# Attention, expert layer and gated layer in one kernel: routing and a weight conversion moved into the last sixth of each attention head

## Chip, cores and metric

One core of one Trainium2 chip. The metric is device time of one execution in microseconds, lower is better; the median of the runs shown is compared. The profile is one separate execution, taken with the hardware profiler.

## What is computed

Three stages, each feeding the next. All inputs are float32 except the three weights of the last stage, which reach the kernel as float64 and are read as pairs of 32-bit words.

```python
# 1 attention: 4 batches x 8 heads, 1152 keys, 64 wide, queries averaged in pairs (576)
scores = (q_pool @ k.T) / 8;  attn = softmax(scores);  x = attn @ v          # x: 2304 x 512
# 2 experts: each token goes to one of 8
e_idx = argmax(x @ w_gate);  gate_w = softmax(x @ w_gate)[e_idx]
out[mask] = gate_w * sigmoid(x @ w_output_gate)[e] * (relu(x[mask] @ w1[e]) @ w2[e])
# 3 gated layer, 1536 wide
out = (silu(x @ w_gate2) * (x @ w_val2)) @ w_out2
```

Outputs are float32. Matrix products are made in float32r, each operand split in a high and a low part (`hi`, `lo`), three products for one.

## The kernel before

Line numbers are those of the profile.

**Attention (32 heads).** A head takes nine blocks of 128 keys. For each, TensorE makes the scores `sb` (L432), ScalarE the exponential `a` (L439), ScalarE or VectorE the high part `ah` (L448), VectorE or GpSimd the low part `al` (L452: GpSimd for blocks 0, 1, 2 and 8), and three blocks later TensorE adds `o` (L470). In the same stretch TensorE and VectorE find the next head's row maxima (`sa` L393, `MX` L397, finished by `m` L402 and placed by `tm` L415), and ScalarE, GpSimd and TensorE prepare the head after that (`ks`, `qs`, `qd`, `vl`, `tk`, `tq`). `sa`, `sb`, `tq`, `tk`, `tx` and the small products of the routing share three PSUM buffers (`ps2`). The order on every engine is written out by hand: the loop over `it` gives each piece a block and a place in it, and `merge` sorts them. Lists that have no fixed place are spread over a fraction of the head.

**Routing.** When the eight heads of a batch are done, `route` makes, on 96 partitions with 6 tokens each, the expert of each token, its rank within the expert (five additions that run along the six tokens, L551, and a product with a triangular matrix, `rk` L556 and L557), the weight, and a row in a table in DRAM, `tbl_d`. Six indirect DMAs on GpSimd's queue write the rows (`put`, L586). `first_steps` then makes `step_e`, the table of the first six expert steps, from three batches. The pieces of batches 0, 1 and 2 are spread evenly over whole heads, 0.02 to 0.98, in heads 9 to 15, 17 to 23 and 25 to 28. Batch 3 is routed during the first three expert steps.

**Start of the experts.** After head 29's pieces (`it == n - 3`), `start_experts` reads `step_e` into registers on SP's queue, loads the token lists `mt` (L134), gathers the tokens of steps 0 and 1 with two indirect DMAs on GpSimd's queue (`xg`, L139), and loads two experts' weights (L150).

**Expert steps.** 23 sure steps of 128 tokens: products `h` (L180), relu `hs`, transposes `t`, products `y` (L899), scaling `ys` (L907), and a scatter to `y_d` on GpSimd's queue (L908). A further group stands behind a branch on a register (L1007), which these inputs do not take.

**Gated layer.** `p` (L1070) over 12 chunks of 128 columns, two at a time, and `o` (L1095). `narrow` turns 128x512 float64 values into float32 by word operations (L236 to L253): four tensor-scalar passes and one two-input pass on VectorE, two activations on ScalarE, two passes on GpSimd. The first two chunks' six units are converted in the last expert steps, in `W1`'s unused buffer as scratch (tile name `W`); what is left of them follows the loop as `after` and stands ahead of the branch. The other 30 units are converted during the gated layer. Loads of `y_d` (L1046) wait for all scatters.

```python
        for ops, slots in zip(made, (tail(2, 8, 12), tail(1, 0, 4), tail(1, 4, 12), tail(0, 0, 12))):
            spread([(0, fn) for fn in ops], slots)
        after = sum(made[4:], [])
```

Of the kernel before, what the change touches and what calls it, by code (L numbers as in the profile page):

```python
# [8 lines left out]
F32 = mybir.dt.float32  # L9
# [28 lines left out]
def kernel(  # L38
# [42 lines left out]
    wide = moe2_w_gate.dtype == I64  # L81

# [10 lines left out]
    iota_e = rt.tile([QP, QT, E], F32, name="iota_e")  # L93
    ebase = rt.tile([QP, QT, E], F32, name="ebase")
# [121 lines left out]
    def narrow(f, part, tile_, to):  # L216
# [21 lines left out]
        ts = nc.vector.tensor_scalar  # L238
        act = nc.scalar.activation
# [10 lines left out]
            lambda: nc.vector.scalar_tensor_tensor(  # L250
                out=t["e"], in0=t["hi"], scalar=-0x80000000, in1=t["e"], op0=ALU.bitwise_and, op1=ALU.bitwise_or
            ),
            lambda: nc.gpsimd.tensor_tensor(out=t["w"], in0=t["w"], in1=t["e"].bitcast(F32), op=ALU.mult),  # L253
# [4 lines left out]
    with ExitStack() as actx:  # L258
# [6 lines left out]
        dup_p = early("dup", 2)  # L265
        one = pool("one", 1)
# [23 lines left out]
        zrow = one.tile([1, DM], F32, name="zrow")  # L290
# [227 lines left out]
        def route(b, ps):  # L518
            s = gs[b]
            G = [QP, QT, E]  # L520
# [6 lines left out]
            lg = rt.tile([QP, QT, 2 * E], F32, name="lg")  # L527
            lo = lg[:, :, 0:E]
            mx = rt.tile([QP, QT, 1], F32, name="gmx")
            d = rt.tile(G, F32, name="gd")  # L530
            ex = rt.tile(G, F32, name="gex")
            oh = rt.tile(G, F32, name="goh")
            mi = rt.tile([QP, QT, 1], F32, name="gmi")
            run = rt.tile(G, F32, name="grun")
            z = rt.tile(G, F32, name="gz")
            ze = rt.tile([QP, QT], F32, name="gze")
            sume = rt.tile([QP, QT], F32, name="gsum")
            meta = rt.tile([QP, QT, 2], I32, name="meta")
            s["oh"], s["meta"] = oh, meta
            flat = lambda t: t.rearrange("p t e -> p (t e)")  # L540
            do(lambda: V.tensor_reduce(out=lg, in_=s["lp"], axis=AX.X, op=ALU.add))
            do(lambda: V.tensor_reduce(out=mx, in_=lo, axis=AX.X, op=ALU.max))

            do(lambda: V.tensor_tensor(out=oh, in0=lo, in1=mx.to_broadcast(G), op=ALU.is_ge))
            do(lambda: V.tensor_tensor(out=oh, in0=oh, in1=iota_e, op=ALU.mult))
            do(lambda: V.tensor_reduce(out=mi, in_=oh, axis=AX.X, op=ALU.min))
            do(lambda: V.tensor_tensor(out=oh, in0=iota_e, in1=mi.to_broadcast(G), op=ALU.is_equal))
# [6 lines left out]
            def ranks():  # L554
                s["rk"] = ps([128, QT * E], "rk")
                nc.tensor.matmul(s["rk"][:QP, :], tri, flat(oh), start=True, stop=False)  # L556
                nc.tensor.matmul(s["rk"][:QP, :], ones, flat(run), start=False, stop=True)  # L557

            do(lambda: V.tensor_tensor(out=d, in0=lo, in1=mx.to_broadcast(G), op=ALU.subtract))
            do(lambda: V.tensor_tensor(out=z, in0=lg[:, :, E:2 * E], in1=oh, op=ALU.mult))  # L560
            do(lambda: V.tensor_reduce(out=ze, in_=z, axis=AX.X, op=ALU.add))
# [5 lines left out]
            do(lambda: V.tensor_reduce(out=sume, in_=ex, axis=AX.X, op=ALU.add))  # L567
            do(lambda: V.tensor_scalar(out=sume, in0=sume, scalar1=1e-9, scalar2=None, op0=ALU.add))
            do(lambda: V.reciprocal(out=sume, in_=sume))
            s["ranks_at"] = len(ops)  # L570
            do(ranks)
            do(lambda: nc.gpsimd.iota(meta[:, :, 0], pattern=[[1, QT]], base=b * SQ, channel_multiplier=QT))
            do(lambda: V.tensor_tensor(out=meta[:, :, 1].bitcast(F32), in0=ze, in1=sume, op=ALU.mult))

            def place():
                sl = rt.tile(G, F32, name="gsl")
                nc.vector.tensor_tensor(out=sl.rearrange("p t e -> p (t e)"), in0=s["rk"][:QP, :], in1=ebase.rearrange("p t e -> p (t e)"), op=ALU.add)
                nc.vector.tensor_tensor(out=sl, in0=sl, in1=s["oh"], op=ALU.mult)
                sf = rt.tile([QP, QT], F32, name="gsf")
                nc.vector.tensor_reduce(out=sf, in_=sl, axis=AX.X, op=ALU.add)  # L580
                si = rt.tile([QP, QT], U32, name="gsi")
                nc.vector.tensor_copy(out=si, in_=sf)
                s["si"] = si

            def put(t):
                i = nc.gpsimd.indirect_dma_start(  # L586
                    out=tbl_d[:, :], out_offset=bass.IndirectOffsetOnAxis(ap=s["si"][:, t:t + 1], axis=0),
# [6 lines left out]
            do(place)  # L594
            for t in range(QT):
                ops.append((500, lambda t=t: put(t)))
            return ops

# [119 lines left out]
        with tc.manual_schedule():  # L718
# [9 lines left out]
            for o, src in ((D + 1, moe_w_gate), (D + 1 + E, moe_w_output_gate)):  # L728
# [8 lines left out]
            nc.vector.memset(zrow, 0.0)  # L737
            nc.gpsimd.memset(tri, 1.0)
            nc.gpsimd.affine_select(
                out=tri, in_=tri, pattern=[[1, QP]], compare_op=ALU.is_gt, fill=0.0, base=0, channel_multiplier=-1  # L740
            )
            fl = nc.gpsimd
            fl.iota(iota_e, pattern=[[0, QT], [1, E]], base=-E, channel_multiplier=0, allow_small_or_imprecise_dtypes=True)
            fl.iota(ebase, pattern=[[0, QT], [NT, E]], base=0, channel_multiplier=0, allow_small_or_imprecise_dtypes=True)
# [9 lines left out]
            nc.sync.dma_start(out=x_d[NT:NT + 1, :], in_=zrow)  # L754
# [7 lines left out]
            pending, events = [], {}  # L762
# [6 lines left out]
            for it in range(-2, n + 1):  # L769
# [29 lines left out]
                if 0 < it < n and it % 2 == 0:  # L799
                    b = (it - 1) // H  # L800
                    if it % H == 0:
                        ops = route(b, ps_a)
                        if b == B - 2:
                            ops += first_steps(ps_a)
# [397 lines left out]
```

## Time and profile before

| | us |
|---|---|
| median of 3 runs (1378.57 to 1382.09) | 1381.45 |
| profiled execution, its own time | 1384.52 |
| its span | 1382.8 |
| PE busy (share of the span) | 1321.7 (96%) |
| DVE busy | 999.7 (72%) |
| ACT busy | 853.7 (62%) |
| POOL busy | 616.0 (45%) |
| PE's share of the chain that ended last | 82% |

The span has three parts: attention up to about 592, experts up to about 895, the gated layer from about 919. A busy share is a mean over parts with different limits; TensorE is the engine to look at in all three, and what counts is where it stands still or runs at the lower of its two clocks.

### The profile page before, as it was taken

Reading aid. Unit: us, or ns where it says so; the run is one execution under the profiler, and the core shown is the slowest. Engines: PE = TensorE matmul, PEld = TensorE weight load, DVE = VectorE, ACT = ScalarE, POOL = GpSimd, SP = SyncE. Lnnn points to the kernel's source line nnn. Section 1 sums busy time; section 2 is a strip of 40 time slices with the busy share of each in tenths; the row PEclk is TensorE's granted clock in tenths of the full one; section 3 lists DMA queues with packets and bytes.
Section 4 is the critical chain, followed back from the end, with each engine's and each line's share of the span. In section 5 each row is a group of like instructions: output and inputs, shape, how many; then the busy total and the mean of one; then the engine's idle time right before and its main releaser. Section 6 shows DMA issues by size and latency. Waiting matters only on the chain.

```text
span 1382.8 us, 22804 instructions
## 1 busy us (share of the span) xinstructions
PE 1321.7 (96%) x8392; PEld 1225.2 (89%) x8392; DVE 999.7 (72%) x1608; ACT 853.7 (62%) x1366; POOL 616.0 (45%) x510
## 2 busy tenths in 40 slices
PE   7999999999999999998999999759999999999998
PEld 6999999999998989877888888549999999999998
DVE  5888888878888898789888888855545555555533
ACT  6888888778876877887888988434332323232211
POOL 7666666676667675306354455521211222122100
PEclk9999999999999999999999999869999999999999
DMA  5333443334333431713545255233111101111011
GB/s 142 87 86 90 109 102 85 82 78 120 87 87 87 121 69 27 276 42 107 184 144 212 79 186 207 94 115 107 39 46 46 46 31 46 47 46 32 16 63 75
DMA packets 96261, 129.58 MB, mean 94 GB/s; under 512 B 47760, under 2 KB 60176, under 8 KB 95762
## 3 DMA queue, kind: packets, MB, share of 16 engines
q1 hardware_dynamic: 91698, 117.31, 29.5%
q0 software_dynamic: 4448, 10.77, 2.3%
q8 instruction: 68, 1.11, 0.4%
q14 instruction: 47, 0.39, 0.1%
HBM read 154.46 MB, written 15.64 MB: 123 GB/s over the span
## 4 chain that ended last, share of the span: by engine, by line
PE 82%; DVE 6%; DMA 5%; issue 3%; ACT 2%; POOL 1%; SPq 0%; POOLq 0%; DVEq 0%
PE p L1070 22%; PE o L470 13%; PE o L1095 11%; PE sb L432 9%; PE h L180 7%; PE y L899 7%; PE sa L393 6%; DMA y_d<-ys,mt 2%; PE tx L493 2%; DVE MX L397 2%; DMA W<-in_moe_w_dram 1%; DVE ah L448 1%; PE tk L367 1%; PE t L888 1%; PE tq L346 1%
## 5 line engine op out<-in xcount | busy, mean ns | idle before, releaser
L397 DVE TENSOR_REDUCE MX<-sa 128x1 f32<-128x576 f32 (+1 forms) x320 | 233.3, 751 | 54.1 <-PE sa L393 50.3
L439 ACT ACTIVATE a<-sb 128x576 f32<-128x576 f32 x288 | 187.8, 652 | 105.3 <-PE sb L432 98.2
L452 POOL TENSOR_TENSOR al<-a,ah 128x576 fp32r<-128x576 f32 x124 | 176.4, 1433 | 131.0 <-DVE ah L448 121.3
L1070 PE MATMUL p<-yh,ah 128*128 128x384 f32 x576 | 195.8, 340 | 0.7 <-ACT yh L1059 0.7
L1070 PE MATMUL p<-yl,ah 128*128 128x384 f32 x576 | 194.4, 338 | 0.0
L1070 PE MATMUL p<-yh,al 128*128 128x384 f32 x576 | 193.9, 337 | 0.0
L470 PE MATMUL o<-ah,vh 128*65 128x288 f32 x576 | 173.8, 302 | 1.2 <-ACT oT L480 1.2
L470 PE MATMUL o<-al,vh 128*65 128x288 f32 x576 | 171.2, 297 | 1.4 <-DVE al L452 1.3
L470 PE MATMUL o<-ah,vl 128*65 128x288 f32 x576 | 170.4, 296 | 0.0
L452 DVE TENSOR_TENSOR al<-a,ah 128x576 fp32r<-128x576 f32 x164 | 141.4, 872 | 20.7 <-ACT ah L448 20.7
L1079 DVE TENSOR_TENSOR u<-p,u 128x384 f32<-128x384 f32 x72 | 40.1, 557 | 147.6 <-PE p L1070 147.6
L393 PE MATMUL sa<-KA,TA 128*128 128x288 f32 (+2 forms) x640 | 142.2, 307 | 4.6 <-DVE MX L397 2.0
L248 POOL TENSOR_TENSOR w<-w,cx 128x512 f32<-128x512 f32 x30 | 38.8, 1295 | 231.2 <-ACT cx L246 231.2
L157 DVE TENSOR_TENSOR w1l<-W,w1h 128x1024 fp32r<-128x1024 f32 x92 | 116.7, 1290 | 23.8 <-ACT w1h L156 19.5
L448 ACT CAST ah<-a 128x576 fp32r<-128x576 f32 x195 | 131.8, 676 | 2.9
L432 PE MATMUL sb<-TA,KA 128*128 128x288 f32 x576 | 125.2, 300 | 0.7 <-DVE MX L397 0.4
L432 PE MATMUL sb<-TB,KB 128*128 128x288 f32 x576 | 124.3, 297 | 0.0
L156 ACT CAST w1h<-W 128x1024 fp32r<-128x1024 f32 x92 | 96.9, 1054 | 33.7 <-PE h L180 29.2
L1070 PEld LDWEIGHTS p<-yh,ah 128*128 128x128 f32 x576 | 108.9, 189 | 4.0 <-ACT yh L1059 1.1
L1070 PEld LDWEIGHTS p<-yh,al 128*128 128x128 f32 x576 | 108.8, 189 | 2.8
L1070 PEld LDWEIGHTS p<-yl,ah 128*128 128x128 f32 x576 | 108.7, 189 | 0.2 <-DVE yl L1060 0.2
L393 PEld LDWEIGHTS sa<-KA,TA 128*128 128x128 f32 (+2 forms) x640 | 98.7, 183 | 11.3 <-DVE MX L397 6.0
(213 smaller groups left out, 3168.8 us busy)
## 6 DMA issues: line engine op xcount, KB each, us to landing
W<-in_moe_w_dram SPq DMA_DIRECT2D x42, 2048.0 KB
kr<-in_k_dram SPq DMA_DIRECT2D x32, 288.0 KB
qr<-in_q_dram SPq DMA_DIRECT2D x32, 288.0 KB
vr<-in_v_dram SPq DMA_DIRECT2D x32, 288.0 KB
KB<-KA SPq DMA_DIRECT2D x31, 288.0 KB
W<-in_moe_w_dram SPq DMA_DIRECT2D x16, 512.0 KB
rb<-in_moe_w_gate_dram SPq DMA_DIRECT2D x10, 512.0 KB
rb<-in_moe_w_val_dram SPq DMA_DIRECT2D x10, 512.0 KB
```

What stands on the lines that cost most here:

```text
L156: nc.scalar.copy(out=hi, in_=W1[p % 2][:, c, :])
L157: nc.vector.tensor_tensor(out=lo, in0=W1[p % 2][:, c, :], in1=hi.bitcast(F32), op=ALU.subtract)
L180: nc.tensor.matmul(s["h"][:, g * 512:(g + 1) * 512], x_[:, c, :], w[:, g * 512:(g + 1) * 512], start=(c == 0 and i == 0), stop=(c == DC - ...
L393: nc.tensor.matmul(ps[:w, c, 0:S // 4], TA[j][0:K_, t * 128:t * 128 + w], KA[j][0:K_, c0:c0 + S // 4], start=True, stop=True,)
L397: nc.vector.tensor_reduce(out=mx[:w, t, hf:hf + 1], in_=ps[:w, :, 0:S // 4], axis=AX.XY, op=ALU.max)
L432: nc.tensor.matmul(ps[:, hf, 0:SQ // 2], w[j][:, c * 128:(c + 1) * 128], t[j][:, hf * (SQ // 2):(hf + 1) * (SQ // 2)], start=first, stop=n ...
L439: nc.scalar.activation(out=a.rearrange("p (a b) -> p a b", a=2), in_=ps[:, :, 0:SQ // 2], func=AF.Exp, scale=0.5 / float(D) ** 0.5,)
L448: (nc.scalar.copy if HI_ACT[c] or i == n - 1 else nc.vector.tensor_copy)(out=ah, in_=a)
L452: (nc.gpsimd if LO_POOL[c] and i < n - 1 else nc.vector).tensor_tensor(out=al, in0=a, in1=ah.bitcast(F32), op=ALU.subtract)
L470: nc.tensor.matmul(s["o", hf][:D + 1, 0:SQ // 2], s[w][:, c, :], s["a"][c][x][:, hf * (SQ // 2):(hf + 1) * (SQ // 2)], start=(c == 0 and p ...
L1070: nc.tensor.matmul(p_, w[:, g, c, :], y_[:, c, :], start=(c == 0 and i == 0), stop=(c == DC - 1 and i == 2),)
L1095: nc.tensor.matmul(ob[t][i], t_[:, ts], w, start=(first and j == 0), stop=(last and j == 2))
```

## The change

1. Conversion of the six early units: each is fetched at the start of head 0, 3, 6, 9, 12 or 15 and converted in three pieces, in the last sixth (0.84 to 0.99) of that head and of the next two, then written to a DRAM tensor `w_d`. The last expert steps only load the finished float32 chunks (`load_chunk`); `after` is gone.
2. `narrow` itself (early units and the 30 later ones): the two GpSimd passes become two VectorE passes, and one activation is folded into one of them.
3. Routing of batches 0 and 1 together, 12 tokens a partition: `sums` at the end of heads 8 and 16, `route` over heads 18 to 21, the twelve `put`s over heads 22 to 25. Batch 2: heads 25 to 27, its six `put`s and `first_steps` over heads 28 and 29. All of it in 0.84 to 0.99 of a head. The running count is one scan in place of copies and additions.
4. Small edits: constants without repetition, a tensor `going` for the scan, the row of zeros of `x_d` from `fill`, no `anew`.

```diff
+    w_d = dram.tile([GF, 128, 3 * DM], F32, name="w_d") if wide else None
...
             lambda: ts(out=t["e"], in0=t["e"], scalar1=896.0, scalar2=0.0, op0=ALU.subtract, op1=ALU.max),
-            lambda: nc.gpsimd.tensor_tensor(out=t["w"], in0=t["w"], in1=t["x"], op=ALU.add),
             lambda: ts(out=t["e"], in0=t["e"], scalar1=254.0, scalar2=float(1 << 23), op0=ALU.min, op1=ALU.mult),
...
-            lambda: nc.gpsimd.tensor_tensor(out=t["w"], in0=t["w"], in1=t["e"].bitcast(F32), op=ALU.mult),
+            lambda: stt(
+                out=t["w"], in0=t["lo"].bitcast(U32), scalar=2.0 ** -52, in1=t["w"], op0=ALU.mult, op1=ALU.add),
+            lambda: nc.vector.tensor_tensor(out=t["w"], in0=t["w"], in1=t["e"].bitcast(F32), op=ALU.mult),
...
-            do(lambda: V.tensor_copy(out=run[:, 0, :], in_=cnt))
-            for t in range(1, QT):
-                do(lambda t=t: V.tensor_tensor(out=run[:, t, :], in0=run[:, t - 1, :], in1=oh[:, t - 1, :], op=ALU.add))
-            do(lambda: V.tensor_tensor(out=cnt, in0=run[:, QT - 1, :], in1=oh[:, QT - 1, :], op=ALU.add))
+            do(lambda: V.tensor_tensor_scan(
+                out=flat(by_e[1]), data0=flat(going[nb - 1]), data1=flat(by_e[0]), initial=0.0, op0=ALU.mult, op1=ALU.add))
+            if b:
+                do(lambda: V.tensor_tensor(out=run, in0=run, in1=per_e(cnt.unsqueeze(1)), op=ALU.add))
+            do(lambda: V.tensor_copy(out=cnt, in_=run[:, T - 1, :]))
...
-                lists = [(pending.pop(0), 0.02, 0.98)] if pending else []
+                lists = []
...
-                        at_, m = gs[b]["ranks_at"], 4 if b == B - 2 else H - 1
-                        cuts = [len(ops) * i // m for i in range(m + 1)]
-                        cuts = [at_ + 4 if at_ < c < at_ + 4 else c for c in cuts]
-                        pending += [ops[a:c] for a, c in zip(cuts, cuts[1:])]
+                if 0 < it < n and it % H == 0:
+                    b = it // H - 1
+                    j, nb = (b, 2) if b < 2 else (0, 1)
+                    rest(it, [(200, lambda: sums(b, j, nb))])
+                    if b == 1:
+                        ops, puts = route(0, 2, ps_a)
+                        over(it + 2, 4, ops)
+                        over(it + 6, 4, puts)
+                    if b == 2:
+                        ops, puts = route(2, 1, ps_a)
+                        over(it + 1, 3, ops)
+                        over(it + 4, 2, puts)
+                        over(it + 4, 2, first_steps(ps_a))
+                if it % 3 == 0 and 0 <= it // 3 < len(units):
+                    f, part = units[it // 3]
+                    fetch, ops, t = narrow(f, part, early_tile, lambda: P["c"].tile([128, DM], F32, name="cw"))
+                    fetch()
+                    ops.append(lambda t=t, f=f, part=part: nc.sync.dma_start(
+                        out=w_d[f, :, part * DM:(part + 1) * DM], in_=t["w"]))
+                    for i, (a, c) in enumerate(((0, 3), (3, 6), (6, len(ops)))):
+                        rest(it + i, [(1, op) for op in ops[a:c]])
+                lists.append((extra.pop(it, []), 0.84, 0.99))
...
+        if wide and f < GF:
+            nc.sync.dma_start(out=r, in_=w_d[f, :, part * DM:(part + 1) * DM])
...
-        for ops, slots in zip(made, (tail(2, 8, 12), tail(1, 0, 4), tail(1, 4, 12), tail(0, 0, 12))):
-            spread([(0, fn) for fn in ops], slots)
-        after = sum(made[4:], [])
+        spread(
+            [(0, lambda f=f, part=part: load_chunk(f, part)) for f in range(GF) for part in range(3)],
+            [(p, c) for p in range(NSURE - 3, NSURE) for c in (4, 5)])
...
-            for fn in after:
-                fn()
```

Three places in the order. The first is VectorE at the end of head 1, where the second piece of a converted unit now stands (`ce` is the exponent word, `rb` the raw words). Before:

```order
L402 TENSOR_REDUCE m<-MX_133 128x5
L452 TENSOR_TENSOR al<-a,ah 128x576 x3
L448 CAST ah<-a 128x576
L397 TENSOR_REDUCE MX_134<-sa 128x1 x5
```

In the change:

```order
L403 TENSOR_REDUCE m<-MX_139 128x5
L453 TENSOR_TENSOR al<-a,ah 128x576 x2
L247 TENSOR_SCALAR ce<-ce 128x512
L248 TENSOR_SCALAR ce<-ce 128x512
L249 SCALAR_TENSOR_TENSOR ce<-rb,ce 128x512
L453 TENSOR_TENSOR al<-a,ah 128x576
L449 CAST ah<-a 128x576
L398 TENSOR_REDUCE MX_140<-sa 128x1 x5
```

A piece now stands between the second and the third `al` of the group, ahead of the cast and of the next head's row maxima.

The second place is where head 29 ends and `start_experts` follows. On VectorE, in the change, the last part of `first_steps` stands there (in the order before, the three writes of `step_e` stood a whole head earlier):

```order
L403 TENSOR_REDUCE m<-MX_139 128x5
L453 TENSOR_TENSOR al<-a,ah 128x576 x2
L639 TENSOR_REDUCE ep<-ge 1x6
L640 TENSOR_TENSOR ge<-ge,nb 1x48
L453 TENSOR_TENSOR al<-a,ah 128x576
L641 TENSOR_REDUCE before<-ge 1x6
L642 TENSOR_TENSOR base<-it_early,before 1x6
L645 TENSOR_SCALAR base<-base 1x6
L648 SCALAR_TENSOR_TENSOR base<-ep,base 1x6
L651 TENSOR_SCALAR step_e<-base 1x6
L652 TENSOR_SCALAR step_e<-ep 1x6
L674 TENSOR_TENSOR step_e<-ep 1x4
```

On GpSimd at the same place, in the change; before, the six `DMA tbl_d` and `MEMSET gap` rows were not here, and the others were in the same order:

```order
L453 TENSOR_TENSOR al<-a,ah 128x576 x4
L318 TENSOR_TENSOR vl<-vr,vh 128x585
L591 DMA tbl_d<-meta,gsi 18560x2
L597 MEMSET gap 1x1
L141 DMA xg<-x_d,mt 128x512 x2
L453 TENSOR_TENSOR al<-a,ah 128x576 x4
```

(the second and third `DMA tbl_d` and `MEMSET gap` are left out). The four `al` of head 29's last block and head 30's first three stand behind both gathers, before and now.

The third place is GpSimd at the end of the sure expert steps. Before:

```order
L908 DMA y_d<-ys,mt 2304x512
L914 MEMSET gap_9050 1x1
L248 TENSOR_TENSOR w<-w,W_1_8350 128x512
L253 TENSOR_TENSOR w<-w,W_1_8350 128x512
L248 TENSOR_TENSOR w<-w,W_1_8350 128x512
L253 TENSOR_TENSOR w<-w,W_1_8350 128x512
L1006 TENSOR_LOAD step_i
```

In the change:

```order
L939 DMA y_d<-ys,mt 2304x512
L945 MEMSET gap_9092 1x1
L1009 TENSOR_LOAD step_i
L1010 COMPARE_AND_BRANCH
```

The branch now follows the last scatter with nothing between.

## Rows read from the trace of the kernel before

**Rows 1.** Windows: us, busy time of each engine, granted clock, DMA share, GB/s.

```profile
297.80:301.20 3.40, 3.40 (x17) 3.32 (x16) 1.44 (x3) 1.48 (x3) 0.69 (x1) 0.50 0.67 117
...
1100.00:1200.00 100.00, 100.00 (x528) 93.83 (x527) 54.17 (x104) 28.49 (x57) 20.62 (x16) 1.00 0.13 43
```

**Rows 2.** Timeline of PE: start, us; first scores of heads 1, 9 and 29.

```profile
37.13 0.43 PE L432 MATMUL sb<-TA,KA 128*128 128x288 f32 x2
...
173.40 0.43 PE L432 MATMUL sb<-TA,KA 128*128 128x288 f32 x2
...
537.98 0.43 PE L432 MATMUL sb<-TA,KA 128*128 128x288 f32 x2
```

**Rows 3.** PE's waits in heads 9 to 28: us in total, times, longest.

```profile
PE tm L415 <- DVE m L402: 8.4, 3, 3.0
```

**Rows 4.** Timelines of DVE and POOL, late in head 15.

```profile
291.71 4.11 DVE L448 CAST ah<-a 128x576 fp32r<-128x576 f32 x1
...
294.52 0.98 POOL L334 TENSOR_TENSOR qd<-qs,qd 96x384 fp32r<-96x384 f32 x1
```

**Rows 5.** Timeline of PE, the last expert steps; in brackets idle time before.

```profile
855.97 0.62 PE L180 MATMUL h<-w1h,xh 128*128 128x512 f32 x2
...
868.34 0.62 PE L180 MATMUL h<-w1h,xh 128*128 128x512 f32 x2
...
887.00 0.80 PE L899 MATMUL y<-w2h,hh 128*128 128x512 f32 x1 [4.73 <-ACT hh L890]
...
895.11 0.40 PE L899 MATMUL y<-w2h,hl 128*128 128x512 f32 x1
```

**Rows 6.** ACT, POOL and SP after the last step; SP's waits; landing times of `y_d`.

```profile
895.55 0.69 ACT L907 ACTIVATE ys<-y,mt 128x512 f32<-128x512 f32 x1 [0.53 <-PE y L899]
...
908.43 1.26 POOL L253 TENSOR_TENSOR w<-w,W 128x512 f32<-128x512 f32 x1 [1.62 <-DVE W L250]
...
911.78 1.76 SPq L1046 DMA_DIRECT2D yr<-y_d  x4
...
SPq L1046 <- DMA y_d<-ys,mt: 9.2, 2, 8.4
...
DMA to landing us min/median/max: 2.9/3.5/8.3
```

**Rows 7.** DVE at the end of plain head 5, and PE in head 6.

```profile
119.53 2.10 DVE L452 TENSOR_TENSOR al<-a,ah 128x576 fp32r<-128x576 f32 x2
122.26 0.76 DVE L452 TENSOR_TENSOR al<-a,ah 128x576 fp32r<-128x576 f32 x1 [0.64 <-ACT ah L448]
...
123.31 1.42 DVE L397 TENSOR_REDUCE MX<-sa 128x1 f32<-128x576 f32 x2
...
124.68 0.42 PE L393 MATMUL sa<-KA,TA 128*128 128x288 f32 x2
```

**Rows 8.** Groups by line and form: count, busy us, mean ns.

```profile
L236 DVE TENSOR_SCALAR cm<-rb 128x512 int32<-128x512 int32 x30 | 12.7, 422 | 0.0
...
L250 DVE SCALAR_TENSOR_TENSOR ce<-rb,ce 128x512 int32<-128x512 int32 x30 | 20.8, 693 | 1.0
...
L586 POOL DMA_INDIRECT tbl_d<-meta,gsi x24 | 33.0, 1373 | 32.1 <-issue 24.2 <-DVE r L498 4.8 <-DVE al L452 2.8
...
L573 DVE TENSOR_TENSOR meta<-gze,gsum 96x6 f32<-96x6 f32 x4 | 0.6, 150 | 0.0
```

**Rows 9.** SP, POOL, DVE and PE where head 30 begins (555.03).

```profile
553.81 6.70 SPq L134 DMA_DIRECT2D mt<-tbl_d  x6
...
555.98 1.01 POOL L139 DMA_INDIRECT xg<-x_d,mt  x1 [8.86 <-DMA mt<-tbl_d]
...
558.27 4.21 POOL L452 TENSOR_TENSOR al<-a,ah 128x576 fp32r<-128x576 f32 x3
...
554.99 0.76 DVE L452 TENSOR_TENSOR al<-a,ah 128x576 fp32r<-128x576 f32 x1 [1.08 <-ACT ah L448]
...
559.76 0.35 PE L470 MATMUL o<-al,vh 128*65 128x288 f32 x1
```

More of the change, by code (lines that the diff above doesn't have):

```diff
@@ L265 @@
         dup_p = early("dup", 2)
+        P["c"] = early("c", 2)
         one = pool("one", 1)
@@ L554, in ranks @@
[L554 to L561, printed above, removed]
+            room = lambda name, w=E, dt=F32: rt.tile([QP, 2 * QT, w], dt, name=name)[:, 0:T]
@@ L562, in route @@
+            do(lambda: V.tensor_reduce(out=one_(ze), in_=z, axis=AX.X, op=ALU.add))
             s["exp_at"] = len(ops)
@@ L570, in route, with ranks @@
+            do(lambda: V.tensor_tensor(out=meta[:, :, 1].bitcast(F32), in0=one_(ze), in1=one_(sume), op=ALU.mult))
             s["ranks_at"] = len(ops)
-            do(ranks)
[L572 to L583, printed above, removed]
+            def ranks():
+                s["rk"] = ps([128, T * E], "rk")
+                rk = s["rk"][:QP, 0:T * E]
+                nc.tensor.matmul(rk, tri, flat(by_e[0]), start=True, stop=False)
+                nc.tensor.matmul(rk, ones, flat(by_e[1]), start=False, stop=True)
+                V.tensor_tensor(out=sl, in0=rk.rearrange("p (e t) -> p t e", e=E), in1=per_e(ebase), op=ALU.add)
@@ L592, in put @@
                 nc.gpsimd.memset(gap, 0.0)
[L594 to L597, printed above, removed]
+            return ops, [(500, lambda t=t: put(t)) for t in range(T)]
         def totals(ops, do, ps, less):
@@ L753 @@
             nc.sync.dma_start(out=tbl_d[:, :].rearrange("(p t) c -> p t c", p=128), in_=fill)
-            nc.sync.dma_start(out=x_d[NT:NT + 1, :], in_=zrow)
+            with nc.allow_non_contiguous_dma("a row of zeros, once"):
+                nc.sync.dma_start(
+                    out=x_d[NT:NT + 1, :].rearrange("o (p f) -> (o p) f", p=4), in_=fill[0:4, 0:DM // 4, 1].bitcast(F32))
             load_v(0)
@@ L760, with over @@
             load_v(2)
-            pending, events = [], {}
+            units = [(f, part) for f in range(GF) for part in range(3)] if wide else []
+            early_tile = lambda nm: P["c"].tile([128, DM, 2] if nm == "rb" else [128, DM], I32, name=nm)
+            extra = {}
+            rest = lambda it, ops: extra.setdefault(it, []).extend(ops)
+            def over(it, heads, ops):
+                for i in range(heads):
+                    rest(it + i, ops[len(ops) * i // heads:len(ops) * (i + 1) // heads])
+            events = {}
             MAX_AT = [(0, 2), (0, 4), (1, 2), (1, 4), (2, 4), (3, 2), (3, 4), (4, 2), (5, 4), (6, 2), (6, 2)]
@@ L822 @@
                     open_first()
-            assert not pending and max(events) == n
+            assert not extra and max(events) == n
             ps_m = lambda shape, name: P["pst"].tile([128, DC * 128], F32, name="t", tag="t")[:, 0:shape[1]]
@@ L832 @@
             at = lambda p, a, b: [(p, c) for c in range(a, b)]
-            ops = route(B - 1, ps_m)
+            spread([(0, lambda: sums(B - 1, 0, 1))], at(0, 2, 3))
+            ops, puts = route(B - 1, 1, ps_m)
             k = gs[B - 1]["ranks_at"]
@@ L838 @@
             spread(ops[j + 2:k], at(1, 6, 8))
-            spread(ops[k:-QT], at(1, 8, 9))
-            spread(ops[-QT:], at(1, 9, 12) + at(2, 0, 4))
+            spread(ops[k:], at(1, 8, 9))
+            spread(puts, at(1, 9, 12) + at(2, 0, 4))
             spread(steps(ps_m), at(1, 4, 12) + at(2, 0, 12))
```

123 lines of the change are left out of this document (51 added, 72 removed).

## Prediction

> **What bounds the kernel.** I read the page's slices first: TensorE stands at nine tenths or ten almost throughout and dips where attention hands over and, deepest, where the experts hand over to the gated layer. So I looked for TensorE's lost time stage by stage: head lengths from the timeline, then waits, then the clock by windows.
>
> Attention: head 1 begins at 37.13 and head 9 at 173.40, so a plain head takes 136.27 / 8 = 17.03 us, and TensorE's work follows itself without a pause. Head 29 begins at 537.98: heads 9 to 28 took 364.58 where twenty plain ones would take 340.6 [rows 2]. **The loss is 24.0 us**, all in the stretch in which the routing of batches 0 to 2 is spread. Three waits, one a batch, make 8.4 of it: TensorE waits for the row maximum `m` [rows 3]. One of them can be followed in head 15. A cast on VectorE, elsewhere 0.45, lasted 4.11, until 295.82; GpSimd's three passes `ks`, `vl`, `qd`, which a `put` had pushed together, had just ended, at 295.50 [rows 4]. After such a stop TensorE runs 3.4 us at a granted clock of 0.50, the lower level of 1.2 GHz, which loses half of that, 1.7 us [rows 1]. The rest is small additions among the row maxima.
>
> End of the experts: a plain step takes 868.34 - 855.97 = 12.37. Then the products `y` of the last step wait 4.73 us for `hh` and start at 887.00; the last starts at 895.11 [rows 5]. ScalarE scales the result from 895.55, and the first load of `y_d` is issued only at 911.78. SP waited 8.4 us for it; the scatter itself is long under way, but GpSimd has conversion passes until 908.43 + 1.26 = 909.69 and reaches the branch and the end of its queue only then [rows 6].
>
> Gated layer: TensorE is busy all of a 100 us window, VectorE 54 [rows 1].
>
> **The change, part by part.** The sum is made against the profiled execution, 1384.52, which is 3.1 above the median of 1381.45; I subtract the sum from the median.
>
> *Tail: 19.2 gained.* Without conversion nothing holds `hs` or `hh`, so step 22 follows in the plain rhythm: its `h` begins at 868.34, the following `y` ends by 880.7, and the last `y` (24 of a step's 48 products) takes at most half a step, 6.2: ended at 886.9, where the trace has 895.5. Then `ys`, 0.69 (887.6), the scatter's landing at its shortest, 2.9, which is late enough for one that runs alone (890.5), and GpSimd's way from its last work to SP's load, 911.78 - 909.69 = 2.1: loads at 892.6 instead of 911.78 [rows 5, 6]. Bounds: 15, if the landing is nearer its longest, 8.3; 21, if the last `y` takes the 5.6 that its products alone need. The six plain loads of finished chunks stand in SP's queue behind waits that are met by then; I cost them at nothing.
>
> *Routing taken out of whole heads: 24.0 gained* [rows 2].
>
> *Pieces in the last sixth: 8 lost.* In a plain head VectorE ends the second `al` at 119.53 + 2.10 = 121.63 and stands until 122.26, 0.64 us, for ScalarE. A piece goes there: 2 x 0.42 in the first, 0.42 + 0.42 + 0.69 = 1.53 in the second, 2 x 0.69 = 1.38 in the third [rows 7, 8]. What is over, 0.2, 0.9 and 0.7, delays the cast and the row maxima. Those end at 123.31 + 1.42 = 124.73; the buffer of the first, free by about 124.0, is wanted by TensorE at 124.68: some 0.65 of cover [rows 7]. So a unit costs about 0 + 0.25 + 0.1 us, six units 2. The nine heads with routing pieces (more, but small operations of 0.15 and up [rows 8]) I put at 0.2 each, 2; the two rank products and the product of the totals hold one of three PSUM buffers, 0.5 each; six heads with three `put`s at 1.37 each [rows 8] occupy GpSimd for 4 us from 120.4, one more than it has free before its next `al`, 0.4 each. Together 7.9. Bounds: 2, if the cover holds everywhere; 20, if each of 27 heads loses what a small addition costs now (the three waits and their clock out, 24.0 - 8.4 - 5.1 = 10.5 over twenty heads, 0.5), and the `put`s one us more each.
>
> *Head 30: 6 lost.* Here the change adds a wait. `step_e` was ready a head before it was read; now its last seven operations stand behind the `al` that ends at 555.7, seven at about 0.19 with their spacing: ready at 557.0. SP's first load of a token list, issued at 553.81 after some 0.8 of register work, must follow it: 4.1 us later. GpSimd's first gather, which waits for that list, began at 555.98, and behind the two gathers stands head 29's last `al`, begun at 558.27, ended 559.7, and wanted at 559.5; TensorE took it at 559.76, with a tenth of a pause [rows 9]. 4.1 later it comes at 563.8: TensorE stops for 4.1 and then runs at the lower clock for some 3.4 us, 1.7 to 2 lost [rows 1]. Bounds: 1, if SP's register work overlaps and `step_e` comes earlier; 8, if the next `al` is late too. The expert weights, loaded behind these lists, come 4 us later, but the first is used more than 10 us after it is in; hidden.
>
> *At nothing:* the 30 later units. VectorE gains 2 x 0.69 and loses none, 1.4 us a unit, 41 us over the gated layer's 460, beside a TensorE that never waits there: 54 busy becomes 63 of 100 [rows 1, 8]. If that cover were gone, the multiplication `u` would be late next. Early fetches and stores, 512 and 256 KB in three heads, go on SP's queue behind loads that are wanted heads later. The scan and the joint routing have no price of their own beyond the pieces.
>
> Sum: -19.2 - 24.0 + 8 + 6 = -29. 1381.45 - 29 = **1352**. With all bounds good, -21 - 24 + 2 + 1 = -42 (1339); all bad, -15 - 24 + 20 + 8 = -11 (1370).
>
> **The rivals.**
>
> *The last sixth is no free place.* TensorE loses in every one of the 27 heads what such an operation costs it now; 20 instead of 8: 1364. For it: pieces of 1.5 are more than the 0.64 of standing time. Against: VectorE stands again, twice, within the next head's first blocks. 0.20.
>
> *Head 30 does not stop and the pieces hide.* Gain 41: 1341, if `step_e` is done early enough for the lists. Against: VectorE's order puts it behind the last `al`. 0.12.
>
> *The tail does not do what it says.* Something beside GpSimd's passes holds the loads, so that only TensorE's 9 us come forward, and the 10 behind stay: 1362. For it: SP's wait is laid to the scatter's landing. Against: GpSimd's passes end 2.1 before the loads. 0.06.
>
> *The cast of head 15, everywhere: slower.* The moved tensor-scalar passes, 0.42 each, are caught as that cast was, 3.7 us lost behind a run of GpSimd's passes, less 0.65 of cover, plus 1.7 of clock: about 4.7 a head. It decides from seven of the twelve heads that hold them (29 / 4.7 = 6.2); in all twelve, +56: 1408. Against: in a plain head GpSimd's last pass is over at 120.4, before the piece begins at 121.6, and its next begins at 123.5. 0.04. The Trainium skill (SBUF — State Buffer, "Who interferes with whom") speaks for such a meeting: a VectorE operation in a two-port mode, or with two SBUF inputs against a GpSimd read, shares a port pair that is held for one whole instruction. By that rule the wait would be one pass, at most 1.45 here, and the twelve heads would give some 10 us, 1362; the trace's 4.11 spans three passes, so the measurement decides for the higher price.
>
> **How the numbers follow.** The forecast has 0.58. 0.3% is 4.1 us, about what a measurement of this kernel can tell from no change. Only the last rival ends at or above the old time: slower 0.04; hardly anything lands within 0.3%: 0.01; faster 0.95. The range takes in the forecast's unknowns and the first three rivals: 1341 to 1366.
>
> **What would show it.** Right: heads 9 to 28 near 17.3 instead of 18.2, no wait of `tm` for `m`; head 30 at about 23 with one stop of about 4 for `al` behind the gathers, and a granted clock of 0.50 after it; the `y` of the last step without a pause, loads of `y_d` 23 to 25 us after the last `h` begins, where the trace has 43; the gated layer as long as before. Wrong: many heads of 17.5 and more, or stops of TensorE in heads 0 to 17, where there were none; loads of `y_d` still 10 us or more after the last scatter begins; a head 30 of 17.

## The result, and the profile after

The changed kernel takes 1357.51 us (median of 4 runs, 1356.24 to 1358.42), the kernel before 1381.77 beside it: a ratio of 0.9829, 95% interval 0.9812 to 0.9846, some 24 us less. The forecast was 1352, with a range of 1341 to 1366. The profiled executions differ by more, 1382.8 and 1354.5 of span, 28.3: that of before lay 2.7 above its median, that of the change 1.3 below.

In the rows, PE is TensorE, DVE VectorE, ACT ScalarE and POOL GpSimd; SPq is SP issuing DMAs. The timeline of PE, first scores of heads 0, 1, 9, 29 and 30 (start, us):

```profile
27.38 0.57 PE L433 MATMUL sb<-TA,KA 128*128 128x288 f32 x1
...
43.48 0.30 PE L433 MATMUL sb<-TA,KA 128*128 128x288 f32 x1
...
181.19 0.43 PE L433 MATMUL sb<-TA,KA 128*128 128x288 f32 x2
...
528.58 0.42 PE L433 MATMUL sb<-TA,KA 128*128 128x288 f32 x2
...
546.12 0.42 PE L433 MATMUL sb<-TA,KA 128*128 128x288 f32 x2
```

From such starts, and those of the first `h` of an expert step, comes the account by stage (differences of starts; "rest" is from the first `h` of the last step, 22, to the end). The kernels e1 to e7 are those of the experiments below.

| us | before | change | e1 | e2 | e3 | e4 | e7 |
|---|---|---|---|---|---|---|---|
| up to head 0 | 20.46 | 27.38 | 19.59 | 28.09 | 19.88 | 19.89 | 20.08 |
| head 0 | 16.67 | 16.11 | 16.68 | 16.42 | 16.35 | 16.85 | 16.61 |
| heads 1 to 8 | 136.27 | 137.71 | 137.67 | 136.26 | 137.59 | 136.40 | 137.63 |
| heads 9 to 17 | 161.79 | 156.51 | 156.45 | 161.66 | 163.50 | 153.59 | 156.59 |
| heads 18 to 28 | 202.79 | 190.88 | 190.85 | 201.31 | 201.71 | 190.69 | 190.82 |
| head 29 | 17.05 | 17.54 | 17.54 | 17.07 | 17.07 | 17.55 | 17.54 |
| head 30 | 17.45 | 21.33 | 21.11 | 17.40 | 17.53 | 21.35 | 17.49 |
| head 31, steps 0 to 21 | 295.86 | 293.20 | 293.35 | 296.25 | 293.87 | 294.59 | 292.77 |
| rest | 514.47 | 493.81 | 494.13 | 514.49 | 493.06 | 514.76 | 494.04 |
| span | 1382.81 | 1354.46 | 1347.37 | 1388.95 | 1360.55 | 1365.67 | 1343.55 |

**The start, which the prediction did not have.** Head 0 begins at 27.38 instead of 20.46. ScalarE stands before the high part of `v`, because its load is late (timeline of ACT; in brackets idle time and what ended it):

```profile
23.02 0.68 ACT L317 CAST vh<-vr 128x585 fp32r<-128x585 f32 x1 [9.71 <-DMA vr<-in_v_dram]
```

On SP's queue the row of zeros (L758) stands just ahead of that load. After:

```profile
8.68 0.82 SPq L758 DMA_DIRECT2D x_d<-fill  x1
9.54 2.15 SPq L307 DMA_DIRECT2D vr<-in_v_dram  x2
11.80 10.11 SPq L299 DMA_DIRECT2D kr<-in_k_dram  x1
```

Before, the row was one piece of 2 KB, and the same issue of `kr` took 1.26:

```profile
9.26 0.30 SPq L754 DMA_DIRECT2D x_d<-zrow  x1
9.61 1.36 SPq L306 DMA_DIRECT2D vr<-in_v_dram  x2
11.07 1.26 SPq L298 DMA_DIRECT2D kr<-in_k_dram  x1
```

In the change the row is read from every second word of `fill`, so it goes as 512 packets of 4 bytes, 128 from each of four partitions. The DMA view of 10 to 11 us shows 275 packets, all small; in 12 to 21, when the loads behind them should run, the DMA engines are hardly busy (last row: packets, MB, share of 16 engines):

```profile
DMA packets 275, 0.00 MB, mean 1 GB/s; under 512 B 275, under 2 KB 275, under 8 KB 275
...
DMA packets 986, 0.25 MB, mean 28 GB/s; under 512 B 986, under 2 KB 986, under 8 KB 986
...
q1 hardware_dynamic: 986, 0.25, 12.0%
```

In the same 9 us the kernel before moves five times as much:

```profile
DMA packets 3110, 1.31 MB, mean 145 GB/s; under 512 B 2886, under 2 KB 2886, under 8 KB 3110
```

**Heads 9 to 28** take 528.58 - 181.19 = 347.39 us, 17.37 a head, where before they took 364.58 [rows 2] and the forecast said near 17.3. The three waits of `tm` for `m` [rows 3] are gone. Two more casts like that of head 15 [rows 4] stand in DVE's timeline of before, in heads 23 and 27, where one takes 0.45 elsewhere (with POOL's passes beside the first):

```profile
436.12 4.10 DVE L448 CAST ah<-a 128x576 fp32r<-128x576 f32 x1
436.14 1.44 POOL L330 TENSOR_TENSOR ks<-kr,ks 128x576 fp32r<-128x576 f32 x1
437.52 1.44 POOL L317 TENSOR_TENSOR vl<-vr,vh 128x585 fp32r<-128x585 f32 x1
438.91 0.99 POOL L334 TENSOR_TENSOR qd<-qs,qd 96x384 fp32r<-96x384 f32 x1
...
511.54 3.40 DVE L448 CAST ah<-a 128x576 fp32r<-128x576 f32 x1
```

The first lasts until all three of GpSimd's passes are over; the second stands beside two, `ks` and `vl`; in the change none of these casts on VectorE lasts over 1.7, and one over 1.1. Where PE still waits in heads 9 to 28 (us in total, times, longest):

```profile
PE sa L394 <- DVE MX L398: 2.7, 5, 0.9
```

The two longest of the five, 0.71 and 0.92, lie in heads 9 and 17. They follow heads 8 and 16, in which `sums` falls on a piece of the conversion. DVE where head 8 ends: the third piece (L252, L254) and the sum (L523) make 2.3 us ahead of `al`, where a plain head has 0.64 free [rows 7], and the four row maxima then follow in one run:

```profile
178.39 2.12 DVE L453 TENSOR_TENSOR al<-a,ah 128x576 fp32r<-128x576 f32 x2
180.43 0.68 DVE L252 SCALAR_TENSOR_TENSOR cw<-rb,cw 128x512 f32<-128x512 uint32 x1
181.15 0.69 DVE L254 TENSOR_TENSOR cw<-cw,ce 128x512 f32<-128x512 f32 x1
181.75 0.94 DVE L523 TENSOR_REDUCE lg<-lp 96x96 f32<-96x768 f32 x1
182.62 0.74 DVE L453 TENSOR_TENSOR al<-a,ah 128x576 fp32r<-128x576 f32 x1
183.28 0.45 DVE L449 CAST ah<-a 128x576 fp32r<-128x576 f32 x1
183.65 2.80 DVE L398 TENSOR_REDUCE MX<-sa 128x1 f32<-128x576 f32 x4
```

**Head 30** stops as forecast: `step_e` is written at 547.69, the first list is asked for at 548.84, 2.7 after the head began (before: 1.2 ahead of it [rows 9]), and `al` stands behind both gathers. DVE, SP, POOL and PE:

```profile
547.69 0.14 DVE L674 TENSOR_TENSOR step_e<-ep 1x4 int32<-1x4 f32 x1
...
548.84 6.36 SPq L136 DMA_DIRECT2D mt<-tbl_d  x6
...
550.84 0.98 POOL L141 DMA_INDIRECT xg<-x_d,mt  x1 [7.74 <-DMA mt<-tbl_d]
...
553.09 4.14 POOL L453 TENSOR_TENSOR al<-a,ah 128x576 fp32r<-128x576 f32 x3
...
554.56 0.35 PE L471 MATMUL o<-al,vh 128*65 128x288 f32 x1 [3.24 <-POOL al L453]
```

After it the granted clock is 0.50 (1.2 GHz) for 3.4 us (windows; the third number from the end is the clock). The second row is a stretch of the gated layer:

```profile
555.00:558.40 3.40, 3.40 (x17) 3.32 (x16) 2.98 (x3) 2.28 (x6) 2.99 (x3) 0.50 0.44 144
...
1100.00:1200.00 100.00, 100.00 (x529) 93.71 (x527) 64.48 (x120) 24.56 (x49) 0.00 (x0) 1.00 0.13 43
```

**The tail.** The last `h` begins at 860.65, the last `y` follow without a pause, and loads of `y_d` are issued 882.45 - 860.65 = 21.8 later; before it was 911.78 - 868.34 = 43.4 [rows 5, 6]. PE, ACT, POOL, SP:

```profile
860.65 0.63 PE L182 MATMUL h<-w1h,xh 128*128 128x512 f32 x2
...
877.94 0.40 PE L930 MATMUL y<-w2h,hl 128*128 128x512 f32 x1
...
878.42 0.69 ACT L938 ACTIVATE ys<-y,mt 128x512 f32<-128x512 f32 x1 [4.93 <-PEq L1010]
...
879.39 0.97 POOL L939 DMA_INDIRECT y_d<-ys,mt  x1 [2.79 <-ACT ys L938]
...
882.45 5.21 SPq L1049 DMA_DIRECT2D yr<-y_d  x6
```

The six loads of finished weights show no cost there, and in the gated layer VectorE is busy 64.48 of 100 us, where the forecast said 63, beside a TensorE that still never waits.

### The profile page after: what moved, and what is told of

It is laid out like the page before. It is cut to its first block, busy times and chain, and to the rows that moved or that the text cites. A ratio compares the mean times of both kernels' runs of the same rounds, so it can differ in the third digit from the quotient of the medians.

```text
span 1354.5 us, 22676 instructions
## 1 busy us (share of the span) xinstructions
PE 1311.4 (97%) x8388; PEld 1220.5 (90%) x8388; DVE 1006.5 (74%) x1641; ACT 832.2 (61%) x1328; POOL 522.8 (39%) x442
## 3 DMA queue, kind: packets, MB, share of 16 engines
HBM read 156.03 MB, written 17.21 MB: 128 GB/s over the span
## 4 chain that ended last, share of the span: by engine, by line
PE 85%; DVE 7%; DMA 3%; ACT 2%; issue 1%; SPq 0%; POOL 0%; DVEq 0%; ACTq 0%; POOLq 0%
PE p L1073 22%; PE o L471 13%; PE o L1098 11%; PE sb L433 9%; PE h L182 8%; PE y L930 8%; PE sa L394 6%; PE tx L494 2%; DVE MX L398 2%; DMA y_d<-ys,mt 1%; PE tk L368 1%; DVE al L453 1%; PE t L919 1%; DMA vr<-in_v_dram 1%; PE tq L347 1%
## 5 line engine op out<-in xcount | busy, mean ns | idle before, releaser
L1085 ACT CAST th<-u 128x384 fp32r<-128x384 f32 x72 | 36.9, 513 | 111.2 <-DVE u L1082 111.2
```

## The experiments

Theory: the account above. The 4-byte row costs about 7 at the start; routing and conversion each gain what the forecast said, separately; head 30 stops because `step_e` is late and `al` stands behind the gathers. Each run is compared with runs of the kernel before on the same chip, whose median was 1381.77 to 1384.96 from one set to the next, so the ratio is what is to be compared.

**e1: the row as 64 packets of 32 bytes**

```diff
-                    out=x_d[NT:NT + 1, :].rearrange("o (p f) -> (o p) f", p=4), in_=fill[0:4, 0:DM // 4, 1].bitcast(F32))
+                    out=x_d[NT:NT + 1, :].rearrange("o (p f) -> (o p) f", p=DM // E), in_=cnt[0:DM // E, :])
```

> The changed kernel; the row of zeros of x_d is written from the zeroed tile cnt, 64 packets of 32 bytes, at the same place of SP's queue, instead of 512 packets of 4 bytes from fill. Theory Z (the 4-byte packets hold the queue, so that the loads of vr behind them land late): the first scores of head 0 begin at about 20.5 instead of 27.4, head 0 takes 16.7 instead of 16.1, all else stays: 6.4 us less, about 1351. Rival S (the start is late for what else the change puts there: the fetch of the first raw weights on the same queue, or GpSimd's memsets of going): first scores still at about 27, 1357.5.

Measured: 1349.15, ratio 0.9754 (0.974 to 0.9769); span 1347.4, 7.1 below the change. First scores at 19.59; everything behind them as in the change. The `kr` behind the row is issued in 1.15:

```profile
8.85 0.50 SPq L758 DMA_DIRECT2D x_d<-cnt  x1
9.41 1.38 SPq L307 DMA_DIRECT2D vr<-in_v_dram  x2
10.88 1.15 SPq L299 DMA_DIRECT2D kr<-in_k_dram  x1
```

The fetch of raw weights and the memsets are still there, so rival S falls.

**e2: the 4-byte row alone, in the kernel before**

```diff
-            nc.sync.dma_start(out=x_d[NT:NT + 1, :], in_=zrow)
+            with nc.allow_non_contiguous_dma("a row of zeros, once"):
+                nc.sync.dma_start(
+                    out=x_d[NT:NT + 1, :].rearrange("o (p f) -> (o p) f", p=4), in_=fill[0:4, 0:DM // 4, 1].bitcast(F32))
```

> The kernel before, with nothing changed but the row of zeros, written as in the change: 512 packets of 4 bytes from fill. Theory Z: first scores of head 0 at about 27.4 instead of 20.5, some 6.4 us more, about 1388, with no conversion and no new memset near. Rival S: no difference, 1381.8, first scores at 20.5.

Measured: 1390.97, ratio 1.0055 (1.0039 to 1.0071), 5.4 to 9.8 us slower; first scores at 28.09, and the issue of `kr` takes as long as in the change:

```profile
11.86 10.66 SPq L297 DMA_DIRECT2D kr<-in_k_dram  x1
```

Adding the row in this form makes the stop, writing it in another form removes it: that the row is the cause is shown. What about its form does it is the question of e6 and e10.

**e3: the conversion alone**

```diff
+                if it % 3 == 0 and 0 <= it // 3 < len(units):
+                    f, part = units[it // 3]
...
+                lists.append((extra.pop(it, []), 0.84, 0.99))
...
-            for fn in after:
-                fn()
```

(with the new `narrow`, `w_d` and e1's row; routing spread as before)

> The kernel before with parts 1 and 2 of the change (conversion of the six early units in the last sixth of heads 0 to 17, narrow without GpSimd), routing as before, and the row of zeros as 64 packets of 32 bytes. Theory: the tail gives its 19 to 22 (loads of y_d 22 to 24 us after the last h begins, where before had 43), the pieces cost about 2 in heads 0 to 17: 18 to 20 less, 1362 to 1364; heads 18 to 28 as before, head 30 about 17. Rival (conversion passes beside the spread routing cost more than alone: VectorE has both in heads 9 to 15): heads 9 to 17 each some 0.5 longer than before, 5 lost, 1367 or more.

Measured: 1363.25, ratio 0.9865 (0.9846 to 0.9883). Loads of `y_d` are issued 889.30 - 867.49 = 21.8 after the last `h`; the rest is 21.4 shorter than before. Heads 9 to 17 take 163.50, 1.7 longer than before, where heads 1 to 8, which have no routing, are 1.3 longer. Single heads pay more than a piece costs alone (11, 12 and 14 are 0.6 to 0.8 longer), others are shorter than before (15 and 16 by 0.3 each); in sum the rival's 5 do not come. Heads 18 to 28 and head 30 are as in e2, which has the old routing too.

**e4: the routing alone**

```diff
-                if it % 3 == 0 and 0 <= it // 3 < len(units):
-                    f, part = units[it // 3]
...
+            for fn in after:
+                fn()
```

(with the old `narrow`, its scratch, and e1's row; routing as in the change)

> The changed kernel without parts 1 and 2: the early units are converted in the last expert steps as before (narrow as before, with GpSimd's passes), routing as in the change, row of zeros as 64 packets of 32 bytes. Theory: the routing gives 24 in heads 9 to 28, its pieces cost 3 to 6 of it, head 30 about 4 (a stop of 3 for al behind the gathers): 14 to 17 less, 1365 to 1368; loads of y_d 43 us after the last h begins, as before. Rival (routing is no cheaper in the last sixth; what heads 9 to 28 gained came from elsewhere): heads 9 to 28 near 18, 1378 or more.

Measured: 1367.09, ratio 0.9882 (0.9867 to 0.9898). Heads 9 to 28 take 153.59 + 190.69 = 344.28, 17.21 each; head 30 stops as in the change; the loads of `y_d` come 894.42 - 850.91 = 43.5 after the last `h`. So routing and tail are separate gains. Two of the forecast's terms can be taken apart here: the conversion's pieces cost 137.67 - 136.40 + 156.45 - 153.59 = 4.1 us (e1 less e4, heads 1 to 17), and the routing's pieces, beside plain heads of 17.03, 0.3 in heads 9 to 17, 3.4 in 18 to 28 and 0.5 in head 29.

**e8: the old tail without GpSimd's passes** (e4 with the new `narrow`; pieces where they were)

```diff
-            lambda: nc.gpsimd.tensor_tensor(out=t["w"], in0=t["w"], in1=t["x"], op=ALU.add),
...
-            lambda: nc.gpsimd.tensor_tensor(out=t["w"], in0=t["w"], in1=t["e"].bitcast(F32), op=ALU.mult),
+            lambda: stt(
+                out=t["w"], in0=t["lo"].bitcast(U32), scalar=2.0 ** -52, in1=t["w"], op0=ALU.mult, op1=ALU.add),
+            lambda: nc.vector.tensor_tensor(out=t["w"], in0=t["w"], in1=t["e"].bitcast(F32), op=ALU.mult),
```

> The kernel with the routing moved but the early units converted in the last expert steps (1367.09), with the changed narrow: GpSimd's two passes of a unit become VectorE's; where the pieces stand is as before. Theory (two things made the old tail: GpSimd's passes ahead of the branch, some 10 to 12 us, and the last y, which wait for hh and start 9 us late): loads of y_d come about 10 earlier, the wait of y for hh stays: 1355 to 1359. Rival (all of the tail is the conversion's place, whichever engine does it: VectorE then ends as late, and the gated layer waits for its split weights): 1364 or more.

Measured: 1358.84, ratio 0.9823 (0.981 to 0.9837); the rest is 7.7 shorter than in e4, of some 20.6 that moving the conversion gives (e1 against e4). The time is as expected, the way to it is not quite. GpSimd is done early: its last scatter (POOL) is issued at 875.62. The loads (SP) still wait for the branch, and the engine that comes to it last is now VectorE: the profile puts a wait of 5.3 of these loads down to VectorE at the branch (L1022), and VectorE's last pass ends at 884.20 + 0.69 = 884.89:

```profile
875.62 1.39 POOL L924 DMA_INDIRECT y_d<-ys,mt  x1 [3.38 <-DVE W L248]
...
884.20 0.69 DVE L253 TENSOR_TENSOR w<-w,W 128x512 f32<-128x512 f32 x1
...
885.53 5.15 SPq L1061 DMA_DIRECT2D yr<-y_d  x6
```

The wait of `y` for `hh`, 4.7 in e4, falls to pieces of at most 1.4. The other 12.9 go only when the pieces go: 6.9 are the last `y`, which end at 874.57, 24.6 after their `h` instead of 17.7, the rest is the branch. One of the delays looks like that of the casts of before, on a pass that takes 0.69 elsewhere. DVE and POOL in e8:

```profile
868.45 2.87 DVE L248 SCALAR_TENSOR_TENSOR W<-W 128x512 int32<-128x512 int32 x1
...
867.81 2.96 POOL L889 TENSOR_TENSOR w2l<-W,w2h 128x1024 fp32r<-128x1024 f32 x1 [10.79 <-ACT w2h L887]
```

**e5: `step_e` a head earlier** (against e1)

```diff
-                        over(it + 4, 2, first_steps(ps_a))
+                        over(it + 3, 2, first_steps(ps_a))
```

> Against the changed kernel with the row of zeros as 64 packets (1349.15): first_steps is spread over heads 27 and 28 instead of 28 and 29, nothing else. Theory (head 30 stops because step_e comes behind the last al of head 29): SP issues the first token list about when head 30 begins minus 1, as before, instead of 2.7 after it; the stop of 3.2 for al behind the gathers and the 3.4 at half clock go, head 30 takes 17.4 instead of 21.1; heads 27 to 29 together within 0.5 of now: 3.5 less, about 1345.5. Rival (the lists wait for the table's last rows, whose three puts end in the last sixth of head 29): the lists land at most 1 us earlier, head 30 stays at 20 or more, 1348 or more.

Measured: 1347.7, ratio 0.9742 (0.9729 to 0.9756). Both were partly right. Head 30 takes 18.74 instead of 21.11; but SP's wait for `step_e` in e1 is replaced by one for the table's last rows. The queue's waits of e1, then of e5, and the stop that is left (PE in e5):

```profile
SPq L130 <- DVE step_e L674: 2.5, 1, 2.5
```

```profile
SPq L136 <- DMA tbl_d<-meta,gsi: 1.5, 1, 1.5
```

```profile
546.30 0.34 PE L471 MATMUL o<-al,vh 128*65 128x288 f32 x1 [1.40 <-POOL al L453]
```

And head 28, which now has the sums of `first_steps` and the last routing piece behind it, takes 18.32 instead of 17.29. Head 30 gains 2.4, heads 18 to 28 lose 1.3 (192.15 instead of 190.85). Of the 3.5, the medians leave 1.5, and by the ratios, whose intervals overlap, even that is not clear of noise.

**e7: the gathers in the middle of head 30** (against e1, `step_e` as late as in the change)

```diff
-        gather(0)
-        gather(1)
...
+                if it == n - 2:
+                    lists.append(([(1, lambda: gather(0)), (1, lambda: gather(1))], 0.45, 0.75))
```

> The same kernel of 1349.15 with step_e as late as in the change, but the two gathers of the first experts' tokens stand on GpSimd's queue in the middle of head 30 (0.45 to 0.75) instead of ahead of the al of head 29's last block. Theory (the late lists hurt only because al stands behind the gathers on GpSimd's queue): head 30 takes 17.4 to 17.8 instead of 21.1, the first step of the experts starts as before relative to head 31: 3.5 less, about 1345.5. Rival (TensorE or VectorE wait for something else that comes late with step_e): head 30 stays above 20, 1348 or more.

Measured: 1345.33, ratio 0.9726 (0.9712 to 0.9739), span 3.8 below e1's. Head 30 takes 17.49. The lists are as late as ever (SP, last row), but GpSimd makes its `al` first:

```profile
541.44 4.19 POOL L451 TENSOR_TENSOR al<-a,ah 128x576 fp32r<-128x576 f32 x3 [5.20 <-DVE ah L447]
...
547.69 0.99 POOL L139 DMA_INDIRECT xg<-x_d,mt  x1
...
541.96 6.39 SPq L134 DMA_DIRECT2D mt<-tbl_d  x6
```

The lateness of `step_e` harms only through the order of GpSimd's queue: shown. By its median this kernel is the fastest of all, 37.5 us below the kernel before.

**e6 and e10: half and a quarter of the row in 4-byte packets** (256 with 32 of 32 bytes; 128 with 48; shown are the 4-byte lines of e6, then of e10, the others come as a second DMA)

```diff
+                    out=x_d[NT:NT + 1, 0:DM // 2].rearrange("o (p f) -> (o p) f", p=2), in_=fill[0:2, 0:DM // 4, 1].bitcast(F32))
...
+                    out=x_d[NT:NT + 1, 0:DM // 4].rearrange("o (p f) -> (o p) f", p=4), in_=fill[0:4, 0:DM // 16, 1].bitcast(F32))
```

> The changed kernel, half of the row of zeros as 256 packets of 4 bytes, half as 32 packets of 32 bytes. Theory (each 4-byte packet takes its time, and the queue behind it waits for the sum): SP's issue of kr behind it lasts about 5 us instead of 10.1 (1.2 with 64 packets), first scores of head 0 at about 23.5, about 3.5 us more than with 64 packets: 1352.5. Rival (any such transfer stops the queue for a fixed time): first scores at 27, 1357.

> The changed kernel, a quarter of the row of zeros as 128 packets of 4 bytes, the rest as 48 packets of 32 bytes. Half a row cost nearly the whole price (first scores at 26.97). Theory now (a stop of fixed length, whatever the number of packets): first scores at about 27, 1356. Rival (the price grows with the packets, but steeply at first): first scores at 22 to 25, 1351 to 1354.

Measured: 1356.55 (0.9804, 0.9791 to 0.9818) with 256 packets, first scores at 26.97; 1353.73 (0.9778, 0.9758 to 0.9798) with 128, first scores at 23.50. With 512 they stood at 27.38, with none at 19.59. My first theory (each packet its price) fails at the half, the second (a fixed stop) at the quarter: by the total of packets, the price rises and then hardly any more. The edits allow a second reading, which I had overlooked. They also set how many packets come from one partition of `fill`: 128 from each of four partitions in the change, 128 from each of two in e6, 32 from each of four in e10. By that count 128 cost 7.8 and 7.4, and 32 cost 3.9. From the change to e6 the total halves at the same count per partition, and the price falls by only 0.4; that speaks for the count per partition. But no run lowers that count alone (256 packets from eight partitions would), so which of the two sets the price is not shown. SP's issue of the `kr` behind them, e6 and e10:

```profile
12.13 7.56 SPq L299 DMA_DIRECT2D kr<-in_k_dram  x1
```

```profile
11.69 6.14 SPq L299 DMA_DIRECT2D kr<-in_k_dram  x1
```

**e9: the 4-byte row at the start of head 2** (against e7; the row at its old place is left out)

```diff
+                if it == 2:
+                    with nc.allow_non_contiguous_dma("a row of zeros, once"):
+                        nc.sync.dma_start(
+                            out=x_d[NT:NT + 1, :].rearrange("o (p f) -> (o p) f", p=4), in_=fill[0:4, 0:DM // 4, 1].bitcast(F32))
```

> The kernel with the gathers in the middle of head 30 (1345.33), the row of zeros again as 512 packets of 4 bytes, but issued at the start of head 2, ahead of loads that are wanted three heads later. Theory (the packets cost only through what waits behind them at that moment): the issue behind it lasts some 10 us, first scores of head 0 at about 20, no head longer by more than 0.3: 1345 to 1346. Rival (the queue also carries the copies KB and TB that the next head needs, and they come late): one stop of TensorE in head 3 or 4, 1349 or more.

Measured: 1350.54, ratio 0.9749 (0.973 to 0.9768), slower than e7. The rival is right: the first scores come at 20.04, but the queue also carries copies that the next head waits for (the one waited for is `TA`, not `KB` or `TB`). The issue of `kr` behind the row lasts 3.22 here, not some 10. Head 3 takes 19.56 instead of 17.21, with one stop of PE:

```profile
74.25 0.50 PE L392 MATMUL sa<-KA,TA 128*128 128x288 f32 x2 [2.33 <-DMA TA<-TA]
```

So the row costs 2.4 there, not 7. The other 2.9 between the spans of e9 and e7 lie in the first expert steps (0 to 3: 53.25 and 50.39). These vary from 50.4 to 53.8 between the kernels with the changed routing, and nothing here tells what sets them.

## Why the prediction was right and where it failed

- **Sign and range: right**; the forecast was 5.5 too low. In the profiles, stage by stage, the change gave 28.3 where the sum said 29; e1, which is the change without the unforeseen start, gave 35.4. That 28.3 stands so near 29 is luck: 6.4 lost at the start was made up by head 30 (2.1 cheaper than forecast), by the stages up to the last step (2.7 shorter, not forecast) and by the end (20.7 instead of 19.2). The median moved by 24.3 only. The sum was read off a profile 3.1 above its median and taken from the median, which takes it that a median run loses as much; no run shows whether it does.
- **"At nothing": failed.** Among the small edits, "the row of zeros of `x_d` from `fill`" got no price, neither in the sum nor as a rival. It cost 6.9 at head 0, of which head 0 gave 0.6 back. What I overlooked is that its 2 KB now go as 512 packets, and that `vr`, for which the first head waits, stands behind them on SP's queue. The early fetches and stores that I did price at nothing cost nothing that shows: in heads 1 to 29 of e1, every wait of TensorE over 0.25 us is for VectorE.
- **Tail, -19.2: right in mechanism, a little small.** The way from the last `h` to the loads is 21.6 shorter (43.4 less 21.8; the gated layer behind it is 1.0 longer, so the table's rest shows 20.7). The last `y` end 17.7 after their `h`, where I took 18.6, and scatter and branch take 4.1, where I took 5.7. The 21.8 is a little under the 23 to 25 that I named as a sign. e8 corrects one thing: taking the passes off GpSimd gives only 7.7 of 20.6; conversion ahead of the branch holds the loads on VectorE as it does on GpSimd. Two bounds of this term do not follow from their reasons: 5.6 instead of 6.2 for the last `y` makes 19.8, not 21, and a landing of 8.3 makes 13.8, not 15.
- **Routing, -24.0, and pieces, +8.** Heads 9 to 28 gave 17.2 net. All pieces cost 8.7: 1.4 in heads 1 to 8, 347.39 - 340.6 = 6.8 in heads 9 to 28, 0.5 in head 29. The sum was right, its division less so. The routing's cost some 4, not 6. The six units cost 4.1, not 2 (e1 less e4): a second piece 0.33 and a third 0.14, seen in the head that follows, where I took 0.25 and 0.1; and about 1.5 more in the two meetings with `sums`, which I had not looked for. There TensorE stops in heads 9 and 17, for 0.71 and 0.92. Stops in heads 0 to 17 were one of my signs of being wrong, and these two are real, if small. That there were none before is wrong too: one of the three waits of [rows 3] is that of head 15.
- **Head 30, +6: right in place and mechanism, too dear.** A stop of 3.24 instead of 4.1, 3.9 in all: beyond the stop 0.6 is left, where I took 1.7 to 2 for the lower clock. e5 shows a second wait, for the table's last rows, just beneath the one I named.
- **The rivals.** The pieces cost 0.3 a head on average, so the first rival's 0.7 is out. The second wanted `step_e` early, which it is not. The third falls with the 21.8 us. The fourth, the cast of head 15 everywhere, has a mechanism that the traces bear out and fell for the reason given against it: none of the 42 VectorE passes of the conversion in attention runs beside a pass of GpSimd, and none lasted 1 us. In e8, where one runs beside a GpSimd pass, it lasted 2.87. The port rule (the Trainium skill, "SBUF — State Buffer", "Who interferes with whom") lets the later of the two wait for one whole instruction: the 2.87 beside one pass of 2.96 agrees, the 4.11 and 4.10 of before, beside three passes, do not.
- **Not foreseen, in the change's favour:** the first expert steps are 2.1 shorter; as they vary by as much between these kernels, I claim nothing from it.

## What to carry to other kernels

Price every edit that touches a queue, also a 2 KB one: count its packets, in all and from one partition, and name the first thing behind it that an engine waits for. A piece fits into a free place of the order only as long as no other piece has been put there: draw up for each head what falls together. And where a late result is not needed for long, look at what stands behind its reader on that reader's queue; moving the reader (e7) took away the whole stop, hurrying the result (e5) a part of it.

## What the hardware showed that was not expected

The 4-byte packets themselves are quick: 275 of the 512 pass in one us. It is the ordinary loads behind them, in packets of 256 bytes (986 packets, 0.25 MB), that then run at 28 GB/s for 9 us instead of 145. Single packets are not slower: 12.0% of 16 engines' 9 us over 986 packets is 18 ns each, as in the kernel before (94.9% of the engines' 2 us over 1707 packets, from 11 to 13 us). Between them the engines stand idle. In e9 the loads behind the row come at 25 GB/s (56 to 66 us), but there the packets under way fill 83.0% of the engines' time, so the two traces do not agree on where the loads are held.

128, 256 and 512 such packets delay the first scores, against e1, by 3.9, 7.4 and 7.8 us; 64 packets of 32 bytes, one from each of 64 partitions, do not. The Trainium skill ("DMA: Bandwidth & Descriptors", "Why small descriptors are slow (HBM only)") puts a fixed overhead of about three cycles on each packet. No run here shows that overhead by itself, and it says nothing of the stop behind the packets; the measurement decides.

What holds those loads up stays open: short writes to DRAM, 4-byte reads of SBUF, or many packets from few partitions would all fit, and it was not tried to part them.
